# First transfers issued in halves from two queues, and two score steps as 64 by 64 products

## The chip, the cores and the metric

The kernel runs on one core of one Trainium2 chip. The time is the device time of one execution in microseconds (us); several runs are taken and their median is given. One execution is also recorded by the hardware profiler, and all rows below are from that recording. Engines are named as in the profile: PE is the matrix engine, PEld its weight loads, DVE, ACT and POOL the vector, scalar and GpSimd engines, SP the engine that issues the transfers (SPq in the rows).

## The reference, cut to what matters

A decayed linear attention is followed by two pairs of dense layers. Only the attention is touched by the change.

```python
# q, k, v: (2, 8, 768, 64); gamma has one value a head
state = zeros((B, H, D, D))
for t in range(S):
    state = gamma * state + einsum('bhd,bhe->bhde', k[:, :, t], v[:, :, t])
    y[:, :, t] = scale * einsum('bhd,bhde->bhe', q[:, :, t], state)
x = y as (1536, 512)
h = x @ w1_in;  x = (h * tanh(softplus(h))) @ w1_out     # 512 -> 2048 -> 512
h = x @ w2_in;  out = (h * cos(h)) @ w2_out
```

## The kernel before

The recurrence is computed in 12 chunks of 128 positions (6 for each of the 2 batches), all 8 heads of a chunk together. One chunk's input is a row block of 128 partitions by 2048 columns of f32, 1 MB: columns 0 to 1023 hold q and k transposed ("qk", 512 KB; partitions 0 to 63 belong to one head of each pair, 64 to 127 to the other), 1024 to 1535 hold v and 1536 to 2047 hold k (256 KB each). For chunk g PE has four steps, written here with a letter and the chunk's number:

- S(g), `att_scores`, L329: 8 products of 64 by 128 weights with 128 columns, the scores of all heads. PE runs an f32 product in two passes, so that the rows count 16. Two products run side by side, on the upper and the lower half of the array.
- O(g), `att_out`, L384: the masked scores `p` (DVE, L336) times v.
- U(g), `att_update`, L345: k times the decayed v, `vd`, into the running state. `vd` is made by POOL (L305) for chunks 0, 3, 6, 8 and 10 and by ACT (L308, 8 instructions) for 1, 2, 4, 7 and 9.
- I(g), `att_inter`, L374: the state of the chunk before times the decayed q, `qd` (POOL, L313 and L316), as 64 by 64 products, four side by side.

PE's order is fixed by hand: 24 products with zeros (L794) that keep it at work while the first data come, S(0), 8 more products with zeros, S(1), O(0), U(0), S(2), O(1), I(1), S(3), U(1), O(2), I(2), U(2), S(4), O(3), U(3), I(3), S(5) and so on. At the end of the chunks stand O(9), U(9), I(9), S(11), O(10), U(10), I(10), O(11), I(11), and then the first products of the dense layers (L431). The order of SP's transfers is fixed by hand too. The first ones are the constants (146 KB, L765; DVE grows the mask of `p` from them, POOL the factors of `qd`), qk of chunk 0, v0, qk1, k0, qk2, v1, qk3, k1; from there on v and k of a chunk come in one transfer of 512 KB. Each transfer counts on one of 8 semaphores, in turn. The order on DVE, ACT and POOL is made by a small planner (`Plan.order`) from estimated costs; a transfer's cost there is 0.00142 us a column for chunks 0 to 2.

Of the kernel before, what the change touches and what calls it, by code (L numbers as in the profile page):

```python
# [10 lines left out]
F32 = mybir.dt.float32  # L11
F32R = mybir.dt.float32r
# [6 lines left out]
B, H, S, D = 2, 8, 768, 64  # L19
DM, DFF = 512, 2048  # L20
C = 128
# [3 lines left out]
BLK = 512  # L25
# [8 lines left out]
IN_G = (8, 9)  # L34
H_ATT = {(0, 0, 0): "s", (0, 1, 0): "h0", (0, 0, 1): "y", (0, 1, 1): "h0"}
VD_ACT = (1, 2, 4, 7, 9)
ST_ACT = (7, 9)
QD_DVE = ()

# [32 lines left out]
class Plan:  # L72
# [15 lines left out]
    def op(self, engine, cost, fn, *args, needs=(), uses=(), new=None):  # L88
        n = len(self.ops)
        uses = list(uses)  # L90
        before = set(needs)
        reuse = None
        if new is not None:
            key, bufs, *tag = new
            line = self.lines.setdefault(tag[0] if tag else key[0], [])
            if line:
                before.add(self.owner[line[-1]])
            if len(line) >= bufs:
                reuse = line[-bufs]
            line.append(key)  # L100
            self.owner[key] = n
            uses.append(key)
        for key in uses:
            if self.owner.get(key, n) != n:
                before.add(self.owner[key])
            self.users.setdefault(key, set()).add(n)
        if engine in self.given:
            before |= {self.last[engine]} if engine in self.last else set()
            self.last[engine] = n
        att = fn.__name__.startswith("att") or fn.__name__ in ("start_up", "zeros", "load_consts")  # L110
        self.ops.append(dict(engine=engine, cost=cost, fn=fn, args=args, before=before, reuse=reuse, att=att))
        return n
# [64 lines left out]
def retention_two_mlps(ctx: ExitStack, tc: tile.TileContext, qkv, w1i, w1o, w2i, w2o, consts, out):  # L177
    nc = tc.nc
# [6 lines left out]
    g_p = ctx.enter_context(tc.tile_pool(name="g", bufs=3))  # L185
# [81 lines left out]
    att = {}  # L267
# [10 lines left out]
            x_t[m, j] = x_p.tile([128, 2, KD, BLK], F32R, tag="x", name="x")  # L278
        return x_t[m, j]

    def att_load(g, lo, hi, eng=nc.sync):
        if not att:
            t = x_p.tile([128, 2, KD, BLK], F32R, tag="x", name="qkv")
            for n in range(2):
                att[n] = t[:, n].rearrange("p a b -> p (a b)").bitcast(F32)
        elif g in IN_WO and g not in att:
            t = wo_p.tile([128, 2, 2, 512], F32R, tag="wo", name="qkv")
            att[g] = t.rearrange("p a b c -> p (a b c)").bitcast(F32)
        elif g in IN_G and g not in att:
            t = g_p.tile([128, 2, 2, BLK], F32R, tag="g", name="qkv")  # L290
            att[g] = t.rearrange("p a b c -> p (a b c)").bitcast(F32)
        elif g not in att:
            att[g] = att_p.tile([128, 2048], F32, tag="qkv", name="qkv", bufs=3)
        eng.dma_start(out=att[g][:, lo:hi], in_=qkv[g, :, lo:hi])  # L294

    def qk_of(g):
        return att[g][:, 0:1024].rearrange("p (a q b) -> p a q b", a=NPAIR, q=2)

    def att_vd(g, part):
# [3 lines left out]
        d = decv[:, g % NCH, :]  # L303
        if g not in VD_ACT:
            nc.gpsimd.tensor_mul(out=vd[g], in0=v, in1=d.unsqueeze(2).to_broadcast([128, H, D]))  # L305
# [13 lines left out]
    def att_scores(g):  # L319
        qk = qk_of(g)  # L320
        if g == 1:
            both = ps_p.tile([128, 2, NPAIR, C], F32, tag="y", name="ps_s")
            ss = [both[:, e] for e in range(2)]
        else:
            ss = [ps_p.tile([128, NPAIR, C], F32, tag="s", name="ps_s", bufs=3) for _ in range(2)]
        for a in range(NPAIR):
            for e in range(2):
                h = slice(D * e, D * e + D)
                nc.tensor.matmul(ss[e][:, a, :], qk[h, a, 1, :], qk[h, a, 0, :], start=True, stop=True)  # L329
        s_t[g] = ss  # L330

    def att_mask(g, e):
# [17 lines left out]
    def att_state(g):  # L350
        state[g] = att_p.tile([128, NPAIR, D], F32, tag="st", name="st")
        u, by = total[g // NCH], back[:, g % NCH, :]
        if g not in ST_ACT:
            nc.vector.tensor_mul(out=state[g], in0=u, in1=by.unsqueeze(2).to_broadcast([128, NPAIR, D]))
# [180 lines left out]
    op = plan.op  # L535
# [48 lines left out]
    def chunk(g):  # L584
        return ("qkv", max(g, 1))

    def chunk_loads(g, cuts, queue=nc.sync):
        key = chunk(g)
        for lo, hi in zip(cuts, cuts[1:]):
            n = op(  # L590
                "SP", (hi - lo) * (0.00142 if g < 3 else 0.00122), att_load, g, lo, hi, queue,
                uses=[key], new=None if key in plan.owner else (key, 3, "x" if g < 2 else "wo" if g in IN_WO else "g" if g in IN_G else "qkv"),
            )
            for part, last in (("qk", 1024), ("v", 1536), ("k", 2048)):
                if lo < last and hi > last - 512:
                    at.setdefault((part, g), []).append(n)

    def chunk_pre(g):
        c = g % NCH
        key = chunk(g)  # L600
        on_act = g in VD_ACT
        if c + 1 < NCH:
            at["vd", g] = [
                op(
                    *(("ACT", 0.98) if on_act else ("POOL", 1.15)), att_vd, g, part, needs=at["v", g] + at["dec"],
                    new=None if part else (("vd", g), 2), uses=[key, ("vd", g)],
                )
                for part in range(2 if on_act else 1)
            ]
        if c > 0:  # L610
            name, cost, eng = ("DVE", 0.72, nc.vector) if g in QD_DVE else ("POOL", 1.95, nc.gpsimd)
            at["qd", g] = op(
                name, cost, att_qd, g, eng, needs=at["qk", g] + at["decq"], new=(("qd", g), 2), uses=[key]
            )
# [4 lines left out]
    def chunk_scores(g):  # L619
        s = [("s", g, e) for e in range(2)]  # L620
        if g == 1:
            s = [("s", g)] * 2
            at["s", g] = op("PE", 1.05, att_scores, g, needs=at["qk", g], new=(s[0], 1, "y"), uses=[chunk(g)])
        else:
            first = op(None, 0.0, nothing, new=(s[0], 3, "s"))
            at["s", g] = op("PE", 1.05, att_scores, g, needs=at["qk", g] + [first], new=(s[1], 3, "s"), uses=[chunk(g), s[0]])
        for e in range(2):
            at["p", g, e] = at["p", g] = op(
                "DVE", 0.71, att_mask, g, e, needs=[at["s", g]] + at["mask"],
                new=None if e else (("p", g), 2), uses=[s[e], ("p", g)],  # L630
            )

    def chunk_update(g):
        c = g % NCH
        if c + 1 == NCH:
# [6 lines left out]
        at["st", g] = op(  # L642
            *(("ACT", 1.0) if g in ST_ACT else ("DVE", 0.43)), att_state, g, needs=[at["u", g]], new=(st, 2), uses=[u],
        )
# [106 lines left out]
    few_t = []  # L751
# [7 lines left out]
        late_h_p = ctx.enter_context(tc.tile_pool(name="late_h", bufs=1, space=PSUM))  # L759
        o_p = ctx.enter_context(tc.tile_pool(name="o", bufs=2, space=PSUM))  # L760

    def load_consts():
        t = g_p.tile([128, 2, 2, BLK], F32R, tag="g", name="few").rearrange("p a b c -> p (a b c)").bitcast(F32)
        few_t.append(t)
        nc.sync.dma_start(out=t[:, 0:292], in_=consts[:, 0:292])  # L765

    def few(lo, n):
        return few_t[0][:, lo : lo + n]
# [22 lines left out]
    def zeros(n, tag):  # L791
        ps = ps_p.tile([128, 256], F32, tag=tag, name="ps_w")
        for _ in range(n):
            nc.tensor.matmul(ps, zero, zero[:, 0:1].to_broadcast([128, 256]), start=True, stop=True)  # L794

    def start_up():
        nc.vector.memset(zero, 0.0)
        nc.vector.memset(quarter, 0.25)
        nc.vector.memset(magic, MAGIC)
        nc.scalar.activation(out=spare, in_=quarter, func=AF.Copy, scale=quarter)  # L800
        zeros(2 * WARM, "u")

    at["close"] = op(None, 0.0, close)
    op("PE", 5.5, start_up)
    load = op("SP", 0.4, load_consts, new=("few", 3, "g"))
    chunk_loads(0, (0, 1024))
    for g in range(2):
        chunk_loads(g, (1024, 1536))
        chunk_loads(g + 1 + g, (0, 1024))
        chunk_loads(g, (1536, 2048))  # L810
        if g == 0:
            chunk_loads(2, (0, 1024))

    def later_loads(gs):
        for g in gs:
# [30 lines left out]
    for n in range(2):  # L846
        chunk_pre(n)
        chunk_scores(n)
        if n == 0:
            op("PE", 0.9, zeros, 8, "u")  # L850
    for n in range(NCHK):
        if 0 < n < NCHK - 1:
            chunk_pre(n + 1)
# [116 lines left out]
```

## Time and profile before

| what | us |
|---|---|
| median of 3 runs (571.49 to 572.43) | 571.52 |
| the profiled execution's own time | 571.26 |
| its span, first to last instruction | 569.5 |
| its mean granted PE clock, as a share of full speed | 1.000 |

The span of the recording is shorter than the execution's time by what lies before the first and behind the last instruction. Sums that are made on the recording are set against 571.26.

### The profile page before, as it was taken

Reading aid. Unit: us, or ns where it says so; the run is one execution under the profiler, and the core shown is the slowest. Engines: PE = TensorE matmul, PEld = TensorE weight load, DVE = VectorE, ACT = ScalarE, POOL = GpSimd, SP = SyncE. Lnnn points to the kernel's source line nnn. Section 1 sums busy time; section 2 is a strip of 40 time slices with the busy share of each in tenths; the row PEclk is TensorE's granted clock in tenths of the full one; section 3 lists DMA queues with packets and bytes.
Section 4 is the critical chain, followed back from the end, with each engine's and each line's share of the span. In section 5 each row is a group of like instructions: output and inputs, shape, how many; then the busy total and the mean of one; then the engine's idle time right before and its main releaser. Section 6 shows DMA issues by size and latency. Waiting matters only on the chain.

```text
span 569.5 us, 7240 instructions
## 1 busy us (share of the span) xinstructions
PE 565.0 (99%) x3052; PEld 469.0 (82%) x3052; DVE 384.4 (67%) x420; ACT 226.8 (40%) x268; POOL 97.7 (17%) x74
## 2 busy tenths in 40 slices
PE   8999999999999999999999999999999999999997
PEld 6888888888888888888888888888888888888886
DVE  6689899652465527563487976898498894765462
ACT  2565443331312302304326466366246354354240
POOL 6770001111110201111101111122010311010000
PEclk9999999999999999999999999999999999999999
DMA  8982154421042200312022120303004100000203
GB/s 295 403 352 83 70 218 148 148 103 46 1 147 75 74 1 7 142 74 75 0 75 75 48 100 1 147 1 147 1 0 148 39 36 1 0 1 0 75 37 112
DMA packets 15008, 49.90 MB, mean 88 GB/s; under 512 B 1664, under 2 KB 2048, under 8 KB 14976
## 3 DMA queue, kind: packets, MB, share of 16 engines
q1 hardware_dynamic: 14976, 49.44, 23.6%
q8 instruction: 24, 0.39, 0.3%
q14 instruction: 8, 0.07, 0.0%
HBM read 46.29 MB, written 3.15 MB: 87 GB/s over the span
## 4 chain that ended last, share of the span: by engine, by line
PE 98%; DMA 1%; SPq 0%; DVE 0%; issue 0%
PE ps_h L431 46%; PE ps_o L454 46%; PE ps_y L384 2%; PE ps_s L329 2%; DMA qkv<-qkv_dram 1%; PE ps_y L374 1%; PE ps_u L345 1%; SPq L294 0%; DVE acc L520 0%; SPq L765 0%
## 5 line engine op out<-in xcount | busy, mean ns | idle before, releaser
L431 PE MATMUL ps_h<-x,wi 128*128 128x512 f32 x1152 | 264.8, 389 | 0.0
L431 PEld LDWEIGHTS ps_h<-x,wi 128*128 128x128 f32 x1152 | 216.2, 188 | 45.0 <-issue 0.2
L454 PE MATMUL ps_o<-wo,g 128*128 128x512 f32 (+1 forms) x588 | 132.5, 385 | 0.0
L454 PE MATMUL ps_o<-g,wo 128*128 128x512 f32 x576 | 132.4, 389 | 0.0
L454 PEld LDWEIGHTS ps_o<-wo,g 128*128 128x128 f32 x588 | 108.9, 188 | 22.0
L454 PEld LDWEIGHTS ps_o<-g,wo 128*128 128x128 f32 x576 | 108.1, 188 | 22.4
L262 POOL TENSOR_TENSOR wo<-mag,wo 128x1024 fp32r<-128x1024 f32 x14 | 35.8, 2559 | 211.4 <-ACT wo L248 158.4
L497 DVE TENSOR_TENSOR g<-mish,g 128x1024 fp32r<-128x1024 f32 x24 | 33.4, 1393 | 55.0 <-ACT g L493 55.0
L513 DVE TENSOR_TENSOR acc<-ps_o,acc 128x1024 f32<-128x1024 f32 x35 | 42.8, 1222 | 34.6 <-PE ps_o L454 34.4
L262 POOL TENSOR_TENSOR wi<-mag,wi 128x1024 fp32r<-128x1024 f32 x12 | 30.3, 2526 | 193.1 <-ACT wi L248 193.1
L464 ACT ACTIVATE mish<-ps_h 128x1024 f32<-128x1024 f32 (+1 forms) x25 | 24.9, 995 | 95.7 <-PE ps_h L431 95.7
L477 DVE SCALAR_TENSOR_TENSOR turns<-whole,turns 128x1024 f32<-128x1024 f32 x24 | 29.3, 1223 | 44.7 <-ACT whole L473 44.7
L469 ACT ACTIVATE turns<-ps_h,quarter 128x1024 f32<-128x1024 f32 x24 | 26.7, 1113 | 65.4 <-PE ps_h L431 65.1
L239 DVE SCALAR_TENSOR_TENSOR mag<-raw,mag 128x1024 uint32<-128x1024 uint32 (+1 forms) x38 | 42.2, 1111 | 1.2
L486 ACT ACTIVATE turns<-turns 128x1024 f32<-128x1024 f32 x24 | 25.5, 1062 | 34.8 <-DVE turns L483 34.6
L497 DVE TENSOR_TENSOR g<-turns,g 128x1024 fp32r<-128x1024 f32 x24 | 33.2, 1383 | 8.0 <-ACT g L493 8.0
L489 DVE TENSOR_TENSOR turns<-turns,ps_h 128x1024 f32<-128x1024 f32 x24 | 29.2, 1216 | 10.1 <-ACT turns L486 6.8
L254 DVE SCALAR_TENSOR_TENSOR mag<-raw,mag 128x1024 uint32<-128x1024 uint32 x26 | 33.8, 1301 | 0.4
L493 ACT CAST g<-turns 128x1024 fp32r<-128x1024 f32 x24 | 25.1, 1045 | 17.0 <-DVE turns L489 16.8
L248 ACT CAST wi<-mag 128x1024 fp32r<-128x1024 f32 (+1 forms) x20 | 17.4, 872 | 26.5 <-DVE mag L254 22.4
L473 ACT ACTIVATE whole<-turns,magic 128x1024 f32<-128x1024 f32 x24 | 27.7, 1153 | 0.8
L483 DVE TENSOR_SCALAR turns<-turns 128x1024 f32<-128x1024 f32 x24 | 27.0, 1126 | 0.8
(50 smaller groups left out, 326.6 us busy)
## 6 DMA issues: line engine op xcount, KB each, us to landing
qkv<-qkv_dram SPq DMA_DIRECT2D x22, 512.0 KB, 10.0
raw<-w1i_dram SPq DMA_DIRECT2D x16, 512.0 KB, 4.2
raw<-w1o_dram SPq DMA_DIRECT2D x16, 512.0 KB, 4.1
raw<-w2i_dram SPq DMA_DIRECT2D x16, 512.0 KB, 3.7
raw<-w2o_dram SPq DMA_DIRECT2D x16, 512.0 KB, 3.7
out_dram<-acc SPq DMA_DIRECT2D x11, 256.0 KB, 2.1
qkv<-qkv_dram SPq DMA_DIRECT2D x4, 256.0 KB, 7.1
out_dram<-acc SPq DMA_DIRECT2D x2, 128.0 KB, 1.7
```

Of the source, the lines that this page charges most:

```text
L239: nc.vector.scalar_tensor_tensor(out=a, in0=high, scalar=0xC0000000, in1=a, op0=ALU.bitwise_and, op1=ALU.bitwise_or)
L254: nc.vector.scalar_tensor_tensor(out=w_all_of(it, single)[:, ns], in0=raw_t[it][:, ns, :, 0], scalar=29, in1=mag_t[it][:, ns], op0=ALU.log ...
L262: eng.tensor_sub(out=w[:, :, 1], in0=w_all_of(it, single)[:, ns].bitcast(F32), in1=w[:, :, 0].bitcast(F32))
L431: nc.tensor.matmul(h[:, 0 if h_tag(k) == "s" else f % 2, :], w[:, f % 2, a, kk * 128 : (kk + 1) * 128], x[:, b, kk, :], start=(a + b + kk ...
L454: nc.tensor.matmul(ps, lhs, rhs, start=(n == 0), stop=(n == 3 * GF - 1))
L469: nc.scalar.activation(out=t_t[k], in_=h_t[k], func=AF.Identity, scale=INV_2PI, bias=quarter)
L473: nc.scalar.activation(out=n_t[k], in_=t_t[k], func=AF.Identity, bias=magic)
L477: nc.vector.scalar_tensor_tensor(out=t, in0=n_t[k], scalar=MAGIC, in1=t, op0=ALU.subtract, op1=ALU.subtract)
L483: nc.vector.tensor_scalar(out=t, in0=t, scalar1=-0.5, scalar2=0.5, op0=ALU.max, op1=ALU.min)
L489: nc.vector.tensor_mul(out=t_t[k], in0=t_t[k], in1=h_t[k])
L497: nc.vector.tensor_sub(out=g[:, :, 1, :], in0=t_t[k], in1=g[:, :, 0, :].bitcast(F32))
L513: nc.vector.tensor_add(out=acc, in0=o_t[m * NG + G, j, p], in1=acc)
```

## The change

- The constants and qk of chunks 0, 1 and 2 are each loaded by two transfers, one for partitions 0 to 63 (UPPER, issued by SP) and one for 64 to 127 (LOWER, issued by ACT). k0 as a whole is issued by ACT too. ACT issues its five in `start_up`, ahead of its first activation: constants, qk0, qk1 (LOWER each), k0, qk2 (LOWER).
- SP's order is now: constants, qk0, qk1 (UPPER each), v0, qk2 (UPPER), v1, qk3, k1. So v0 stands behind qk1, where it stood ahead of it.
- The planner's cost of these transfers is 0.0013 us a column, halved for a half.
- S(0) and S(11) are 16 products of 64 by 64 weights, the keys in two halves, in the order in which all four quarters of the array are used in turn.
- 4 products with zeros, not 8, stand between S(0) and S(1).

```diff
+SQUARE = (0, 11)
...
-    def att_load(g, lo, hi, eng=nc.sync):
+    early = []
+    issued = set()
+    EVERY, UPPER, LOWER = slice(0, 128), slice(0, 64), slice(64, 128)
+
+    def att_load(g, lo, hi, eng=nc.sync, at_rows=EVERY):
...
-        eng.dma_start(out=att[g][:, lo:hi], in_=qkv[g, :, lo:hi])
+        if (g, lo, hi, at_rows) not in issued:
+            eng.dma_start(out=att[g][at_rows, lo:hi], in_=qkv[g, at_rows, lo:hi])
+            issued.add((g, lo, hi, at_rows))
...
         for a in range(NPAIR):
-            for e in range(2):
-                h = slice(D * e, D * e + D)
-                nc.tensor.matmul(ss[e][:, a, :], qk[h, a, 1, :], qk[h, a, 0, :], start=True, stop=True)
+            for keys in (slice(0, D), slice(D, C)) if g in SQUARE else (slice(0, C),):
+                for e in range(2):
+                    h = slice(D * e, D * e + D)
+                    nc.tensor.matmul(
+                        ss[e][keys, a, :], qk[h, a, 1, keys], qk[h, a, 0, :], start=True, stop=True, skip_group_check=True,
+                    )
...
-                "SP", (hi - lo) * (0.00142 if g < 3 else 0.00122), att_load, g, lo, hi, queue,
+                "SP", (hi - lo) * (0.0013 if g < 3 else 0.00122) * share, att_load, g, lo, hi, queue, at_rows,
...
+            if queue is not nc.sync:
+                early.append((g, lo, hi, queue, at_rows))
...
     def start_up():
+        load_consts(nc.scalar, LOWER)
+        for load in early:
+            att_load(*load)
         nc.vector.memset(zero, 0.0)
...
-    chunk_loads(0, (0, 1024))
     for g in range(2):
-        chunk_loads(g, (1024, 1536))
-        chunk_loads(g + 1 + g, (0, 1024))
-        chunk_loads(g, (1536, 2048))
-        if g == 0:
-            chunk_loads(2, (0, 1024))
+        chunk_loads(g, (0, 1024), at_rows=UPPER)
+        chunk_loads(g, (0, 1024), nc.scalar, LOWER)
+    chunk_loads(0, (1024, 1536))
+    chunk_loads(0, (1536, 2048), nc.scalar)
+    chunk_loads(2, (0, 1024), at_rows=UPPER)
+    chunk_loads(2, (0, 1024), nc.scalar, LOWER)
+    chunk_loads(1, (1024, 1536))
+    chunk_loads(3, (0, 1024))
+    chunk_loads(1, (1536, 2048))
...
         if n == 0:
-            op("PE", 0.9, zeros, 8, "u")
+            op("PE", 0.45, zeros, 4, "u")
```

## Rows read from the trace of the kernel before

**Rows 1.** The page: what each engine was busy, and the chain's shares.

```profile
PE 565.0 (99%) x3052; PEld 469.0 (82%) x3052; DVE 384.4 (67%) x420; ACT 226.8 (40%) x268; POOL 97.7 (17%) x74
...
PE 98%; DMA 1%; SPq 0%; DVE 0%; issue 0%
```

**Rows 2.** The chain in order of time: start, length, what.

```profile
2.10 6.57 DMA qkv<-qkv_dram
...
8.71 1.16 PE ps_s L329 x16
...
38.45 0.60 PE ps_y L374 x16
39.05 1.09 PE ps_s L329 x16
```

**Rows 3.** Timeline of the first 11 us: start, length, instructions, [idle before <- releaser].

```profile
5.86 0.27 PE L794 MATMUL ps_w<-zero 128*128 128x256 bf16 x1
...
6.07 1.16 PE L329 MATMUL ps_s<-qkv 64*128 64x128 f32 x16
7.16 1.06 PE L794 MATMUL ps_w<-zero 128*128 128x256 bf16 x8
```

**Rows 4.** Timeline of the first 11 us, the other engines.

```profile
7.26 1.29 DVE L336 TENSOR_TENSOR p<-ps_s,cst 128x512 f32<-128x512 f32 x2 [0.26 <-PE ps_s L329]
7.44 1.04 POOL L305 TENSOR_TENSOR vd<-qkv,cst 128x512 f32<-128x512 f32 x1
...
10.62 0.60 PEld L345 LDWEIGHTS ps_u<-vd,qkv 128*64 128x64 f32 x16
...
10.94 0.58 ACT L398 CAST x<-ps_y 128x512 fp32r<-128x512 f32 x1 [8.63 <-PE ps_y L384]
```

**Rows 5.** Transfers: SP's issues of v0, k0, qk2 and v3 with k3.

```profile
1.64 0.42 SPq L294 DMA_DIRECT2D qkv<-qkv_dram  x1
...
2.58 0.43 SPq L294 DMA_DIRECT2D qkv<-qkv_dram  x1
3.05 0.58 SPq L294 DMA_DIRECT2D qkv<-qkv_dram  x1
...
8.69 0.33 SPq L294 DMA_DIRECT2D qkv<-qkv_dram  x1
```

**Rows 6.** Transfers, size and us to landing: v0, k0, qk2; the constants; later weights.

```profile
qkv<-qkv_dram SPq DMA_DIRECT2D x1, 256.0 KB, 5.2
qkv<-qkv_dram SPq DMA_DIRECT2D x1, 256.0 KB, 6.7
qkv<-qkv_dram SPq DMA_DIRECT2D x1, 512.0 KB, 7.5
few<-consts_dram SPq DMA_DIRECT2D x1, 146.0 KB, 2.3
raw<-w1i_dram SPq DMA_DIRECT2D x16, 512.0 KB, 4.2
```

**Rows 7.** Stretches: busy time of each engine; last the clock, DMA share, GB/s.

```profile
2.00:8.00 6.00, 6.00 (x45) 4.32 (x42) 4.43 (x11) 0.31 (x2) 4.38 (x10) 1.00 0.94 274
8.00:10.00 2.00, 1.51 (x22) 1.17 (x22) 0.63 (x2) 0.00 (x0) 1.59 (x3) 1.00 1.06 420
10.00:20.00 10.00, 10.00 (x200) 8.81 (x198) 7.84 (x14) 5.59 (x19) 7.42 (x11) 1.00 1.02 392
20.00:30.00 10.00, 10.00 (x201) 8.75 (x199) 6.83 (x13) 4.76 (x15) 8.18 (x12) 1.00 1.03 410
```

**Rows 8.** Timeline around U(7): ACT's `vd` of chunk 7 and the step that reads it.

```profile
29.47 2.02 ACT L308 ACTIVATE vd<-qkv,cst 128x64 f32<-128x64 f32 x8 [1.44 <-DMA qkv<-qkv_dram]
...
31.46 0.63 PE L345 MATMUL ps_u<-vd,qkv 128*64 128x64 f32 x16
```

**Rows 9.** I(9), the first round and the first three rounds of four 64 by 64 passes.

```profile
38.38 0.34 PE L374 MATMUL ps_y<-qd,st 64*64 64x128 f32 x4
...
38.38 0.56 PE L374 MATMUL ps_y<-qd,st 64*64 64x128 f32 x12
```

More of the change, by code (lines that the diff above doesn't have):

```diff
@@ L585, in chunk, with chunk_loads @@
         return ("qkv", max(g, 1))
-    def chunk_loads(g, cuts, queue=nc.sync):
+    def chunk_loads(g, cuts, queue=nc.sync, at_rows=EVERY):
         key = chunk(g)
+        share = (at_rows.stop - at_rows.start) / 128
         for lo, hi in zip(cuts, cuts[1:]):
             n = op(
-                "SP", (hi - lo) * (0.00142 if g < 3 else 0.00122), att_load, g, lo, hi, queue,
+                "SP", (hi - lo) * (0.0013 if g < 3 else 0.00122) * share, att_load, g, lo, hi, queue, at_rows,
                 uses=[key], new=None if key in plan.owner else (key, 3, "x" if g < 2 else "wo" if g in IN_WO else "g" if g in IN_G else "qkv"),
             )
+            if queue is not nc.sync:
+                early.append((g, lo, hi, queue, at_rows))
             for part, last in (("qk", 1024), ("v", 1536), ("k", 2048)):
@@ L760, in close, with load_consts @@
         o_p = ctx.enter_context(tc.tile_pool(name="o", bufs=2, space=PSUM))
[L762 to L765, printed above, removed]
+    def load_consts(eng=nc.sync, at_rows=UPPER):
+        if not few_t:
+            t = g_p.tile([128, 2, 2, BLK], F32R, tag="g", name="few")
+            few_t.append(t.rearrange("p a b c -> p (a b c)").bitcast(F32))
+        eng.dma_start(out=few_t[0][at_rows, 0:292], in_=consts[at_rows, 0:292])
     def few(lo, n):
```

## The prediction

> **What bounds the kernel now.** I read the page first: PE is busy for 99% of the span, and the chain that ended last runs on PE for 98% of it [rows 1]. Next the chain in order of time: ahead of S(1) it follows a transfer, qk1, that was issued at 2.10 and takes 6.57 us; from S(1) at 8.71 on it never leaves PE until the last accumulation [rows 2]. So the 557.8 us from 8.71 to the end of PE's work are PE's own steps without a gap, and a change of the first transfers can win only (a) what starts S(1) and the steps behind it earlier, and (b) what shortens a step. Then the timeline of the start says what else stands ahead of S(1): the last warming product starts at 5.86, S(0) at 6.07, the 8 zero products at 7.16, ending at 8.22 [rows 3]; PE then waits about half a microsecond for qk1. Last come the transfers and the places later on where something with a time of its own, and not one that follows PE, just makes it.
>
> **The change part by part.**
>
> *Zeros and S(0).* The zero products take (1.06 - 0.27)/7 = 0.113 us each at this place [rows 3]; four fewer are 0.45 us. S(0) itself can hardly move: the warming products end where they did, the last begins at 5.86, and whatever qk0's landing adds is within the 0.2 us from there to 6.07. As squares (below) it is 0.05 shorter. So PE could begin S(1) at 8.22 - 0.45 - 0.05, about 7.7, a full microsecond earlier, if its data were there.
>
> *qk1.* In the order of before, 146 + 512 + 256 + 512 KB = 1426 KB stand up to and with qk1; it lands at 2.10 + 6.57 = 8.67 [rows 2]. v0 (914 KB) lands at 1.64 + 5.2 = 6.84, k0 (1682 KB) at 2.58 + 6.7 = 9.28, qk2 (2194 KB) at 3.05 + 7.5 = 10.55 [rows 5, 6]. In the new order v0 is behind, so that 1170 KB stand up to and with qk1. Read off the same curve between 6.84 and 8.67 this is 7.75. With 0.04 us from landing to PE, S(1) begins at about 7.8, 0.9 earlier.
>
> *v0.* This is the price, and it takes most of that back. v0 is now served side by side with k0 behind 1170 KB: its last byte is between 1426 KB (8.67, if it is served first) and 1682 KB (9.28, if the two take turns to the end). I take 9.2, near the second, since the two stand in different queues. Behind v0 hangs POOL's `vd` of chunk 0, which takes 1.04 us [rows 4] and which U(0) reads. In before it was far ahead of U(0), whose weights start to load at 10.62 [rows 4]. Now it is late next: 9.2 + 0.1 + 1.04 + 0.1 = 10.44, so U(0) moves up by only 0.18. With 9.28 it is 0.10; with 8.67 `vd` would be ready at 9.9, and PE's own steps (S(1) at 7.8, 1.16 to O(0) by rows 2, then O(0)) put U(0) at about 10.0, 0.65 earlier. The mask is no limit: `p` of chunk 0 is ready at 7.26 + 1.29 = 8.55 [rows 4], ahead of O(0) at 8.95 or later. Behind `vd` on POOL stands `qd` of chunk 1, pushed back too, but I(1) has room for it: S(2) and O(1) come first.
>
> *The stream of transfers later on.* From 10 us on they move 392 to 410 GB/s with the transfer engines busy all the time [rows 7], so that a landing there is a matter of bytes before it, and from qk2 on the bytes before each transfer are what they were. A step that reads such data can come earlier only by its slack. The tightest that I find is U(7): ACT begins `vd` of chunk 7 when its transfer lands, at 29.47, and has the last of 8 heads at 31.49; U(7) runs from 31.46 to 32.09 and needs that head in its second half [rows 8]. That leaves about 0.2 us. A PE that is 0.2 us ahead just passes; one that is a microsecond ahead is held there, unless the whole stream has moved up.
>
> *Does the stream move up?* From 2 to 8 us it moved 274 GB/s, against 420 from 8 to 10 [rows 7]: at 410 from the start, (6 x (410 - 274))/410 = 2.0 us less. If the slow start were a matter of issuing, two queues would mend it. It does not look so: qk1 is in the queue by 2.53 [rows 5] and lands at 8.67. [...]
>
> *Issue.* ACT has nothing of the chain to do before 10.94 [rows 4], so its five issues, about 0.45 each by SP's [rows 5], 2.2 us in all, are hidden; they would cost from the moment they ran past 10.94. On SP the issues stay short, but an issue waits for the eighth before it: 8.69 stands 0.02 behind the landing of qk1 [rows 5, 2]. ACT's five come first in the count, so v0 waits for the LOWER constants (2.3 us to landing [rows 6], so about 3), qk2 UPPER for qk0 LOWER (about 6), v1 for qk1 LOWER (7.75), qk3 for k0 (9.3). Queued behind on SP are all later chunks. With 4.2 us from issue to landing of a lone 512 KB [rows 6], qk2 would be there at 10.2 and qk3 at 13.5, about when they were; some 768 KB still under way cover the gap. I take it at nothing; without that cover S(2) or S(3) waits some tenths.
>
> *S(11) as squares.* It stands behind I(9), which is made of 64 by 64 products already. I(9) takes 0.60 and S(11) 1.09 to the next start [rows 2]. A further round of four 64 by 64 passes takes (0.56 - 0.34)/2 = 0.11 [rows 9]; S(11) is 8 such rounds, 0.88 if it follows without a break, 0.21 less than now. If it had to start anew as I(9) does, 0.60 + 4 x 0.11 = 1.04, 0.05 less. I take 0.21, since I(9) shows that such rounds follow one another. For S(0), which stands between products of another shape, it is the 0.05 from above, and hidden while S(1) waits for its data.
>
> **The sum.** S(1) could win 0.9, U(0) keeps 0.18, U(7) lets about 0.2 through: -0.2. S(11): -0.2. Together -0.4: 571.26 - 0.4 = 570.9 for a profiled execution. The median of the runs is 0.26 above the profiled one, so 571.52 - 0.4 = **571.1**.
>
> **The rivals.**
>
> 1. *The start gets faster.* The two queues keep the transfer engines as busy from 2 us as from 10. Then qk1 is there by 7.7, v0 well before 8.55, the stream moves up by up to 2.0 and U(7) with it; PE's own steps are the limit: -1.0 for S(1), -0.2 for S(11), 570.3. For it: 274 against 410 GB/s, and shares of the transfer engines below one (0.94) in that stretch. Against it: issuing is long done, and the bytes are the same. Half a gain (0.5 to 0.9) belongs here too.
> 2. *It is hidden anyway.* v0 lands at 9.4, U(0) stays where it was, squares win 0.05: 571.5, no change. For it: the curve gives 9.28, only 0.1 off.
> 3. *Slower: v0 comes late.* Every microsecond by which v0 lands behind 9.4 is one on the path, by POOL's `vd` of chunk 0 and U(0). If transfers of 64 partitions moved a quarter slower in the start, 2 + 1.25 x (9.28 - 2) = 11.1: U(0) at 12.3, 1.7 later, less 0.2 of S(11): +1.5, 573.0. It gets slower by over 0.2% from a landing at about 10.8. Against it: k0 with half of qk2's bytes lands 0.6 us behind qk1, qk2 1.3 behind k0, so smaller transfers as such are no slower; a transfer of half the partitions the trace does not have. [...]
>
> **How the numbers follow.** Forecast (-0.05 to -0.7 around -0.4) 0.55; rival 1, 0.17, of which 0.10 reach 0.2%; rival 2, 0.19; rival 3, 0.09, of which 0.07 pass 0.2%. I use 0.2%, 1.14 us, as about what a measurement of this kernel can tell from no change. The whole possible gain, 1.2 us, just passes that. So faster 0.10, same 0.83, slower 0.07. The range reaches from rival 1's 570.3, with 0.2 for the scatter of the runs, to +0.5 of a mild rival 3: 570.1 to 572.0.
>
> **What would show it.** In the profile after: S(1) near 7.8, behind 4 zero products and a short wait on qk1. U(0) should wait on POOL's `vd`, which itself waited for v0 until about 9.2; a U(0) at 10.0 would show v0 served first, one behind 10.6 the slower case. Transfers from 2 to 8 us near 274 GB/s; near 400 would be the first rival. U(7) should be at or near the end of ACT's `vd`. I(9) and S(11) should take 1.48 together instead of 1.69. The prediction is wrong if the stretch from S(1) to the end has shrunk by more than the 0.2 of S(11), if PE has found a new wait behind U(0), or if the planner's other order on DVE, ACT or POOL makes PE wait in the dense layers, where it never did.

## The result: 0.6% slower

The changed kernel took 575.02 us in the median of 6 runs (574.68 to 575.64), the kernel before 571.61 (571.44 to 572.62, 6 runs beside it). The ratio is 1.0056, with a 95% interval from 1.0044 to 1.0069. The forecast was 571.1, in a range up to 572.0. The profiled execution took 574.96 against 571.26, 3.70 more.

The page of the profile after. PE is still busy for 99% of the span, but 3% of the chain that ended last are now transfers, where it was 1% [rows 1]:

```profile
PE 564.8 (99%) x3080; PEld 468.6 (82%) x3080; DVE 385.1 (67%) x420; ACT 226.9 (40%) x268; POOL 98.0 (17%) x74
...
PE 96%; DMA 3%; ACTq 0%; DVE 0%; issue 0%; SPq 0%
```

The chain of the profile after, in order of time (start, length, what), to be laid beside [rows 2]:

```profile
2.23 7.22 DMA qkv<-qkv_dram
...
9.46 0.33 SPq L300
...
9.84 8.68 DMA qkv<-qkv_dram
...
18.56 1.09 PE ps_y L394 x16
...
20.25 0.75 PE ps_u L355 x16
...
41.58 0.60 PE ps_y L384 x16
42.17 0.87 PE ps_s L337 x32
...
44.54 0.37 PE ps_y L384 x7
44.91 0.18 issue
45.09 0.54 PE ps_y L384 x9
...
47.25 0.90 PE ps_h L441 x3
```

The same chain in the kernel before, at O(2) and at the first products of the dense layers, and the transfer of v2 and k2 there, which was issued at 6.01 (size, us to landing):

```profile
15.78 0.88 PE ps_y L384 x16
...
43.85 32.86 PE ps_h L431 x144
```

```profile
qkv<-qkv_dram SPq DMA_DIRECT2D x1, 512.0 KB, 8.3
```

Before, PE never had to wait again once it had started S(1). Now it waits at O(2), 18.56, for the transfer of v2 and k2, which was issued at 9.84 and lands at 18.52. From there on it runs through as before, 3.1 us late, up to S(11) at 42.17 (39.05 before [rows 2]). S(11) took 0.87 to the next start instead of 1.09. Then, in I(10), stands a break in which PE waited for nothing that the profile shows; with it I(10) took 1.09 instead of 0.60. The first product of the dense layers starts at 47.25, where it was 43.85.

The timeline of PE in the start of the profile after, and POOL's `vd` of chunk 0, beside [rows 3, 4]:

```profile
5.86 0.43 PE L337 MATMUL ps_s<-qkv 64*64 64x128 f32 x2 [0.79 <-DMA qkv<-qkv_dram]
8.06 1.10 PE L337 MATMUL ps_s<-qkv 64*64 64x128 f32 x30 [1.78 <-DMA qkv<-qkv_dram]
9.10 0.62 PE L808 MATMUL ps_w<-zero 128*128 128x256 bf16 x4
9.64 1.16 PE L337 MATMUL ps_s<-qkv 64*128 64x128 f32 x16
10.73 1.09 PE L394 MATMUL ps_y<-p,qkv 128*64 128x128 f32 x16
12.73 0.69 PE L355 MATMUL ps_u<-vd,qkv 128*64 128x64 f32 x16 [0.91 <-DMA qkv<-qkv_dram]
```

```profile
10.40 1.05 POOL L312 TENSOR_TENSOR vd<-qkv,cst 128x512 f32<-128x512 f32 x1 [2.56 <-DMA qkv<-qkv_dram]
```

S(0) ran its first two passes on the UPPER half of qk0 and then waited 1.78 us for the LOWER one. POOL waited for v0, and U(0) waited for k0. Of the row blocks that the steps wait for, each is complete later than before: qk0 at 8.02 (6.00 before), qk1 at 9.45 (8.67), v0 at 10.33 (6.81), k0 at 12.60 (9.32). The reason shows in the stretches of the profile after (busy time of each engine; last the clock, DMA share, GB/s; the share adds up the times of the packets and can pass one), beside [rows 7]:

```profile
2.00:8.00 6.00, 3.50 (x23) 2.37 (x20) 3.69 (x9) 1.58 (x2) 3.85 (x9) 1.00 0.94 219
8.00:10.00 2.00, 1.94 (x40) 1.53 (x42) 0.80 (x2) 0.00 (x0) 0.00 (x0) 1.00 1.07 260
10.00:20.00 10.00, 8.64 (x160) 7.35 (x156) 6.40 (x11) 4.59 (x16) 7.52 (x10) 1.00 1.02 351
20.00:30.00 10.00, 10.00 (x205) 8.57 (x195) 6.93 (x12) 4.19 (x15) 7.60 (x11) 1.00 1.03 413
```

And 8 to 13 us, while most of the halves are under way, first the kernel before, then the change:

```profile
8.00:13.00 5.00, 4.51 (x78) 3.98 (x78) 3.35 (x6) 2.06 (x8) 4.28 (x7) 1.00 1.04 407
```

```profile
8.00:13.00 5.00, 4.03 (x75) 3.29 (x77) 2.58 (x4) 0.59 (x1) 2.45 (x3) 1.00 1.05 249
```

The transfer engines were as busy as before (shares of 0.94 and 1.07, before 0.94 and 1.06), and moved fewer bytes: 260 GB/s in 8 to 10, where it was 420. PE's granted clock is 1.00 in all these stretches, so the clock is no part of it. The last half lands at 13.58, and from 13 us on the rate is the old one (398 from 13 to 20, 389 before).

**Where the 3.70 us are.** v2 with k2 landed 4.2 later than before (18.52 against 14.3); O(2) had 1.4 of slack, so it moved by 2.78 (18.56 against 15.78 in the chain before). ACT's `vd` of chunk 2 starts at that landing too and makes U(2) late by another 0.35. S(11) gives back 0.21. The break in I(10) costs 0.49. The last 0.30 lie behind the last product, in the store of the result.

Of the 4.2 us by which v2 with k2 is late, 2.9 are the stream's: k1, the transfer ahead of it, is 2.85 late (15.96 against 13.11) and the one behind it 3.2. The other 1.3 stand beside a packet of 16 KB of the instruction queue (16.39 to 17.48 in the trace's transfer records): v2 with k2 lands 2.55 behind k1, where such transfers follow one another by 1.2 to 1.3. Before, that packet (13.73 to 14.68) came a transfer later, and the one behind v2 with k2 landed 2.18 after it and had the slack for it. In all 17 traces the first or second landing behind the end of the first such packet, 0.7 to 2.2 us behind it, stands 1.6 to 2.8 us behind the one ahead of it. That the packet causes this no run here shows, and such gaps occur without one too. It moves the place of the loss more than its size: the transfer of chunk 7 is 3.1 late in any case, and an estimate from that and from U(7)'s slack of 0.2 [rows 8] is a loss of 2.9 there. In the kernel with the change's transfers only, below, v2 with k2 landed at 17.21, while the packet was still under way, O(2) did not wait for it, and the dense layers still began 3.0 later than before.

### The profile page after: what moved, and what is told of

It is laid out like the page before. It is cut to its first block, busy times and chain, and to the rows that moved or that the text cites. A ratio compares the mean times of both kernels' runs of the same rounds, so it can differ in the third digit from the quotient of the medians.

```text
span 573.2 us, 7303 instructions
## 1 busy us (share of the span) xinstructions
PE 564.8 (99%) x3080; PEld 468.6 (82%) x3080; DVE 385.1 (67%) x420; ACT 226.9 (40%) x268; POOL 98.0 (17%) x74
## 4 chain that ended last, share of the span: by engine, by line
PE 96%; DMA 3%; ACTq 0%; DVE 0%; issue 0%; SPq 0%
PE ps_h L441 46%; PE ps_o L464 46%; DMA qkv<-qkv_dram 3%; PE ps_y L394 2%; PE ps_s L337 1%; PE ps_y L384 1%; PE ps_u L355 1%; ACTq L300 0%; ACTq L779 0%; DVE acc L530 0%; SPq L300 0%
## 5 line engine op out<-in xcount | busy, mean ns | idle before, releaser
L249 ACT CAST wi<-mag 128x1024 fp32r<-128x1024 f32 (+1 forms) x20 | 17.5, 873 | 26.6 <-DVE mag L255 22.4
```

## The experiments

All times are medians, each with its ratio to runs of the kernel before on the same chip (571.6 to 571.9). GB/s are those of the profiled execution in three stretches; the last column is the landing of v2 with k2 there.

| kernel | us (runs) | ratio, 95% interval | 2:8 | 8:10 | 13:20 | v2 with k2 |
|---|---|---|---|---|---|---|
| before | 571.6 | | 274 | 420 | 389 | 14.3 |
| the change | 575.02 (6) | 1.0056, 1.0044 to 1.0069 | 219 | 260 | 398 | 18.5 |
| halves, one queue | 575.54 (4) | 1.0069, 1.0046 to 1.0092 | 203 | 227 | 367 | 19.1 |
| halves by columns | 574.64 (4) | 1.0049, 1.0033 to 1.0064 | 235 | 409 | 332 | 15.3 |
| squares only | 572.30 (10) | 1.0011, 1.0001 to 1.0021 | 278 | 388 | 411 | 15.1 |
| order, whole, one queue | 572.15 (10) | 1.0005, 0.9995 to 1.0014 | 228 | 425 | 399 | 15.2 |
| the change's transfers only | 574.62 (4) | 1.0045, 1.0032 to 1.0059 | 219 | 249 | 394 | 17.2 |
| even and odd partitions | 573.10 (8) | 1.0021, 1.0010 to 1.0031 | 252 | 411 | 413 | 17.1 |
| S(11) alone | 571.74 (11) | 0.9999, 0.9990 to 1.0007 | 278 | 411 | 416 | 16.0 |
| squares, 8 zeros | 572.07 (11) | 1.0003, 0.9995 to 1.0012 | 288 | 392 | 412 | 15.2 |
| qk2 in two halves | 573.51 (10) | 1.0032, 1.0019 to 1.0045 | 298 | 246 | 404 | 16.2 |
| qk2 in four quarters | 574.10 (6) | 1.0041, 1.0027 to 1.0056 | 292 | 245 | 397 | 15.6 |
| squares S(9) to S(11) | 573.04 (12) | 1.0015, 1.0005 to 1.0025 | 268 | 376 | 415 | 15.7 |
| even and odd, one queue | 575.04 (4) | 1.0054, 1.0038 to 1.0069 | 216 | 378 | 387 | 17.5 |
| weights by row ranges | 572.33 (1) | | 262 | 417 | 416 | 16.4 |
| whole, two queues | 572.98 (10) | 1.0022, 1.0009 to 1.0034 | 317 | 416 | 390 | 13.5 |
| v0 and k0 from ACT | 571.56 (11) | 0.9999, 0.9990 to 1.0008 | 310 | 399 | 396 | 14.4 |

**Which part costs: queues, halves, order or squares.** Three kernels undo one part of the change each, and a fourth has the squares and the 4 zeros alone. The theories were: W, transfers of 64 partitions are slow; Q, two queues served by turns are; S, SP's late issues are.

```diff
-        chunk_loads(g, (0, 1024), nc.scalar, LOWER)
+        chunk_loads(g, (0, 1024), nc.sync, LOWER)      # all halves, and k0, from SP
```

> The changed kernel with the LOWER halves and k0 issued by SP, next to their UPPER halves, and nothing by ACT. Theory W (transfers into 64 partitions move slowly, whoever issues them): the stretch from 2 to 13 us still moves about 240 GB/s, v2 with k2 lands near 18, the time is about 574 to 576. Theory Q (two queues that take turns on the same transfer engines slow each other): from 8 us on about 410 GB/s, v2 with k2 lands near 14.5, about 571.5. Theory S (SP's issues come late, since they wait for the landing of the eighth before): also near 571.5, with the issues of v1, qk3 and k1 by 6 us.

```diff
-        chunk_loads(g, (0, 1024), at_rows=UPPER)
-        chunk_loads(g, (0, 1024), nc.scalar, LOWER)
+        chunk_loads(g, (0, 512))                       # halves by columns
+        chunk_loads(g, (512, 1024), nc.scalar)
```

> The changed kernel with qk of chunks 0 to 2 cut by columns and not by partitions: 128 partitions of 512 columns from SP and as many from ACT; the constants whole, from SP. Queues, counts and order stay. Theory W: about 400 GB/s from 6 us on, v2 with k2 near 14.5, about 571.3. Theory Q: as slow as the change, about 240 GB/s to 13 us, 574 to 576. Theory S: slow by the gaps behind SP's waits alone; the rate is full while both queues have work, about 572 to 573.

```diff
+SQUARE = (0, 11)                                       # on the kernel before
...
-            op("PE", 0.9, zeros, 8, "u")
+            op("PE", 0.45, zeros, 4, "u")
```

> The kernel before with the 64 by 64 products for chunks 0 and 11 and 4 zero products, transfers untouched. All theories: S(1) still waits for qk1 until 8.7; S(11) takes 0.88 behind I(9), so 571.6 - 0.2 = 571.4. If the squares or the fewer zeros carry the loss, it is 573 or more; a break of about 0.5 us in I(10), as in the changed kernel, would show that this belongs to the squares and not to late data.

```diff
-        chunk_loads(g, (0, 1024), at_rows=UPPER)
-        chunk_loads(g, (0, 1024), nc.scalar, LOWER)
+        chunk_loads(g, (0, 1024))                      # whole, all from SP, order of the change
```

> Whole transfers, SP alone, in the changed order (qk0, qk1, v0, k0, qk2, v1, qk3, k1), squares and 4 zeros. The working of the prediction without its halves: S(1) near 7.8, v0 near 8.7 to 9.3, U(0) 0.1 to 0.6 earlier, v2 with k2 near 14.3, about 571.1. If the order itself were the loss: U(0) behind 10.7 and 572 or more.

Halves from one queue are as slow as from two, so Q falls. S falls with it: SP had issued v1 and qk3 by 7.86 there, and from 8 to 10 us full transfer engines (share 1.07) moved 227 GB/s. Whole transfers in the new order, with the squares, are within 0.1% of before, so the loss is in the halves, and the new order has won nothing: qk1 landed at 8.80 there, although v0's 256 KB no longer stood ahead of it. That execution had a slow start, though (228 GB/s from 2 to 8): qk2, with the same bytes ahead of it as before, landed 0.8 late as well (11.37 against 10.56). The squares alone were forecast at 571.4 and took 572.30, 0.1% above before: their trace has a break in I(10) again, of 0.37. Halves by columns kept the full rate from 8 us on (409) and were slow for another reason. Both queues served qk0 among the rest, and its second half came at 7.85; PE idled 1.82 us ahead of S(0), its granted clock fell (0.66 from 8 to 13), and S(1) took 2.01 us instead of 1.09. The stretch of the kernel with halves by columns, clock third from the end:

```profile
8.00:13.00 5.00, 5.00 (x68) 4.14 (x70) 3.02 (x5) 0.00 (x0) 3.29 (x4) 0.66 1.05 406
```

Next, the transfers of the change without its squares, and the squares without its transfers:

```diff
-SQUARE = (0, 11)                                       # on the change
+SQUARE = ()
...
-            op("PE", 0.45, zeros, 4, "u")
+            op("PE", 0.9, zeros, 8, "u")
```

> The transfers of the change (halves of 64 partitions on two queues, the new order) with the score steps and the zeros of before. Theory W (while halves of 64 partitions are under way, the full transfer engines move some 40% fewer bytes, so that v2 with k2 lands near 18.5 and O(2) waits for it): 2:8 near 220 and 8:13 near 250 GB/s, O(2) near 18.6, and the time 2.9 to 3.3 above before, some 574.7, since S(11) gives nothing back. Theory P (the square products set the loss, by PE's shape changes in the start or by PE's own instructions coming late): under 572.5. The break of PE in I(10) should be gone or stand elsewhere if it hangs on the number of PE instructions ahead of it.

```diff
+SQUARE = (11,)                                         # on the kernel before
```

> Transfers and zeros of before; only S(11) is made of squares. If the gain of S(11) stands, 0.2 below before: 571.4. If the break of PE behind it (0.3 to 0.7 us in I(10) where both steps were squares) is a matter of where PE's instructions come from, it moves by the 8 to 12 instructions that are fewer ahead of it, and the time is 571.4 to 572.2.

```diff
+SQUARE = (0, 11)                                       # on the kernel before, 8 zeros kept
```

> Transfers of before, both steps as squares, 8 zeros as before. S(1) at 8.7 to 8.85, since it waits for its data anyway. If the break of PE hangs on the count of PE instructions ahead of it, it stands 4 products earlier than with 4 zeros, at the start of I(10) or in U(10); if it hangs on the moment, it stays about 44 to 45 us. The time 571.3 to 572.3.

The transfers alone cost 2.9 us, as W had it. Only the place moved: the chain of that execution goes over v0, which landed at 12.26, and O(0) waited for it:

```profile
2.89 9.37 DMA qkv<-qkv_dram
...
12.40 1.09 PE ps_y L394 x16
```

S(11) alone gained nothing that can be measured, though it took 0.87 in the profile too; in that execution O(2) waited 0.3 for v2 with k2, which landed at 15.96, 2.5 behind k1 and behind an instruction packet that ended at 14.92. The breaks of PE are taken up below.

**Why halves are slow.** The same two halves as even and odd partitions, from two queues and from one:

```diff
-    EVERY, UPPER, LOWER = slice(0, 128), slice(0, 64), slice(64, 128)
+    EVERY, UPPER, LOWER = slice(0, 128), slice(0, 128, 2), slice(1, 128, 2)
```

> The change as it is, but with the halves as the even and the odd partitions: again 64 partitions to a transfer, the same bytes, queues and order, but spread over all 128. [...] Theory W2 (few rows to a transfer cost, wherever they lie, since each then goes to fewer engines or in other pieces): as slow as the change, 8:13 near 250 GB/s, the time 574.5 to 575.5.

> The even and odd partitions again, all issued by SP, in order. They left 1.4 us of the loss with two queues. If that rest comes from the two queues (SP waits for a landing before it issues v2 with k2, and the halves of qk0 and qk1 land side by side with others): 571.9 to 572.4, the time of whole transfers in this order. If it comes from the transfers being halves (more and shorter ones in the start): again 572.8 to 573.4.

In 8 to 10 us both moved 411 and 378 GB/s, against 260 and 227 for neighbours: the number of partitions is not what cost, but which they were, and W2 falls. The times did not follow the rate: 573.1 and 575.0. From two queues O(2) waited 1.5 us for v2 with k2. The chain of that kernel:

```profile
8.61 8.46 DMA qkv<-qkv_dram
...
17.12 1.09 PE ps_y L394 x16
```

k1 had landed at 14.32, 1.2 later than before; v2 with k2 came 2.75 behind it, again behind an instruction packet (14.89 to 15.82). At the usual 1.2 to 1.3 it would have been there at 15.6, in time for O(2): in the one execution recorded, the rest of the loss hangs on this gap. From one queue the odd half of qk0 landed at 7.84, PE idled 2.04 us ahead of S(0) and the granted clock was 0.66 from 8 to 13, S(1) again 2.01 long; that fits the late qk0 of the halves by columns, not W. That kernel also has a slow stretch from 10 to 13 us (225 GB/s at a share of 0.97), which I can't explain. The halves don't show in it: from 7.84 on they and v0 and k0, 256 KB each, land 0.6 to 0.7 us apart up to the last half at 11.70; it is the whole transfers behind them, v1 and qk3, that take until 13.32 and 15.64.

Then a dose: one transfer of the kernel before, qk2, in halves and in quarters.

```diff
-        eng.dma_start(out=att[g][:, lo:hi], in_=qkv[g, :, lo:hi])
+        for r in range(0, 128, 64 if (g, lo) == (2, 0) else 128):      # 32 for quarters
+            rows = slice(r, r + (64 if (g, lo) == (2, 0) else 128))
+            eng.dma_start(out=att[g][rows, lo:hi], in_=qkv[g, rows, lo:hi])
```

> The kernel before, with one single transfer changed: qk2 (512 KB) as two transfers of partitions 0 to 63 and 64 to 127, both from SP. A third of the bytes that the change moves in halves. Theory W (a range of 64 neighbouring partitions is written at the 249 GB/s of the changed kernel instead of 410): 0.52 MB take 2.1 us instead of 1.3, so the stream behind qk2 is 0.8 later, v2 with k2 lands near 15.2 (hidden, O(2) starts at 15.8), and U(7) with its 0.2 of slack passes on 0.6: 572.3. Theory E (what costs is the first engine-wide start or the use of two queues, not the halves): 571.7, no change.

> The same single transfer as four of 32 neighbouring partitions each. [...] Theory N (the rate falls in proportion to the number of neighbouring partitions): half of the rate of the halves, 4.2 us for qk2, the stream 2.9 later, 574.4. Theory D (each further transfer has a price of its own): twice to three times what the two halves cost over before.

In both the rate fell while qk2 was under way, to 246 and 245 GB/s, and the last part of qk2 landed at 11.35 in both (10.6 before): 32 neighbours were no slower than 64 (P in the run with the weights below), and N falls. The profiled execution of the halves took 572.24, and 572.3 was the forecast; but v2 with k2 landed at 16.22 instead of 15.2 (2.4 behind k1, an instruction packet having ended at 14.27), and O(2), which was to be untouched, waited 0.4. The ten runs reach from there to 575.83, and the medians are 1.2 (halves) and 1.8 (quarters) above those 572.3, so the size of the dose is not shown by the times. In the recorded execution of the quarters (573.84) O(4) waited 0.48 for a transfer that landed at 22.80, 2.8 behind the one ahead of it, 1.7 us after the next instruction packet; S(8) waited for ACT's work on weights that landed at 29.20 (26.86 before). The other executions were not recorded.

Last, the same question where nothing else moves. The weights of the dense layers come in pairs of 512 KB; here they are split in three ways.

```diff
+PARTS = {
+    "i0": (slice(0, 128),),                                    # w1i
+    "o0": (slice(0, 64), slice(64, 128)),                      # w1o
+    "i1": (slice(0, 128, 2), slice(1, 128, 2)),                # w2i
+    "o1": (slice(32, 96), slice(0, 32), slice(96, 128)),       # w2o
+}
...
-            nc.sync.dma_start(out=to, in_=of)
+            for rows in PARTS[it[0] + str(m)]:
+                nc.sync.dma_start(out=to[rows], in_=of[rows])
```

> A measurement on the kernel before, away from the start: the weights of the dense layers come in pairs of 512 KB transfers when nothing else moves, w1i whole as before, w1o as partitions 0 to 63 and 64 to 127, w2i as even and odd partitions, w2o as 32 to 95, then 0 to 31 and 96 to 127. Theory W with P (a range of 64 or 32 neighbours inside one half of the partitions is written at some 250 GB/s, a range with as many partitions from both halves at full rate): the pair of w1o lands some 1.8 us later than a whole pair (1.05 MB at 249 instead of 410 is 4.2 us instead of 2.6), w2i's no later than 0.3, and of w2o the 32 to 95 part runs at full rate and the two others at the slow one. Theory H (64 partitions are slow whichever they are; even and odd ones were quick for another reason): w2i and w2o as late as w1o. Theory S (it belongs to the start alone): all as whole. The time itself 571.4 to 572.4, since the weights have slack there.

Stretches of 7 or 8 us with one pair of 1.05 MB in each, so that the share of the transfer engines' time that the pair took can be compared. The whole pair of w1o, in the profile of the kernel before:

```profile
81.00:89.00 8.00, 8.00 (x37) 6.62 (x36) 7.53 (x12) 4.12 (x5) 0.00 (x0) 1.00 0.35 131
```

The split weights: w1o in halves, w2i even and odd, w2o with its middle half in one piece:

```profile
81.00:89.00 8.00, 8.00 (x37) 6.62 (x36) 7.49 (x14) 3.42 (x5) 0.00 (x0) 1.00 0.54 131
...
292.00:299.00 7.00, 7.00 (x32) 5.79 (x32) 6.05 (x7) 1.77 (x2) 0.00 (x0) 1.00 0.46 152
300.00:308.00 8.00, 8.00 (x37) 6.63 (x36) 4.76 (x3) 5.25 (x5) 2.48 (x1) 1.00 0.50 132
```

For the same bytes the engines need 0.35 x 8 = 2.8 us for whole transfers, 0.54 x 8 = 4.3 for halves of neighbours, 0.46 x 7 = 3.2 for even and odd partitions. w2o, half of it in partitions 32 to 95 and half in the two outer quarters, needs 4.0, and in two other pairs 3.6 and 3.9; the middle between whole and halves is 3.6. So the slowness is not of the start, it went with the range: 131/0.54 = 243 GB/s at full share for partitions 0 to 63 and 64 to 127, 131/0.35 = 374 for all.

The forecast was made of landings, and by them it held in part. From the first issue to the last landing the pair of w1o took 6.7 us (4.4 whole), 2.3 more where 1.8 was forecast; w2i 1.1 more (5.5, whole 4.4) where 0.3 was, as SP needs 0.6 us for each of its four issues; w2o as much as w1o (2.2 more), so that its landings don't show 32 to 95 to be quick. The single packets of 4 KB, one partition's row each, do. In order of their starts, the third 64 packets of a pair (the third transfer of a split pair, if the queue keeps its order) take 159 to 161 ns in the median in whole pairs, in w2i and in all six pairs of w2o, where they are the second 32 to 95, and 287 to 308 in w1o. This also answers a rival: 64 neighbours are read from rows that follow one another in the source, and even or odd ones are not; but 32 to 95 follow one another too, and are quick.

So in these runs the rate went by which partitions a transfer covered: 64 neighbours from 0 or from 64 on were slow (243 GB/s at full share against 374), quarters of 32 like halves (245 and 246 in 8 to 10 us), even and odd ones near whole (3.2 us a pair against 2.8), 32 to 95 quick by their packets (159 to 161 ns). Why it is so no trace here shows.

**Is there anything in a second queue?** Two kernels keep it and drop the halves:

```diff
-    for g in range(2):                                 # on the change
-        chunk_loads(g, (0, 1024), at_rows=UPPER)
-        chunk_loads(g, (0, 1024), nc.scalar, LOWER)
+    chunk_loads(0, (0, 1024))
+    chunk_loads(1, (0, 1024), nc.scalar)               # qk2 whole from ACT too, constants from SP
```

> The change without its halves: constants, qk0, v0, v1, qk3, k1 whole from SP, qk1, k0, qk2 whole from ACT, both score steps as squares and 4 zeros. If the halves are what costs, 3 us of the 3.4 come back: 571.6 to 572.4, with 8:13 near 410 GB/s. If two queues side by side cost something of their own (qk1 from ACT is served beside qk0, which then lands late, PE idles in the start and its granted clock falls), 573 to 575.

```diff
+    chunk_loads(0, (1024, 1536), nc.scalar)            # v0, beside k0; the rest whole from SP
...
-SQUARE = (0, 11)
+SQUARE = ()
```

> What the runs so far point to: whole transfers, constants, qk0, qk1, qk2, v1, qk3, k1 from SP, v0 and k0 from ACT behind its first activation, so that they don't push qk0 back; no square steps, 4 zeros. Theory R (a second queue keeps the transfer engines busier in the start, 317 against 274 GB/s, so that the whole stream is ahead): 2:8 above 300 GB/s, qk0 near 6, qk1 by 8.3, S(1) 0.4 earlier, v2 with k2 by 14: 570.9 to 571.5. Theory T (the bytes of the two queues are served by turns, so that what one transfer wins another loses): qk1 no earlier than 8.7 or qk0 late as in the two-queue run before it (7.8), 571.7 to 573.

The first 6 us moved more here, 317 and 310 GB/s, where the eight recorded executions with SP alone and the first transfers of before moved 262 to 298; v2 with k2 landed 0.8 earlier in the first. With one execution each, that two queues raise the rate is likely and not shown. Neither kernel is faster than before. In the first, qk1 from ACT was served ahead of qk0. The chain of that kernel:

```profile
1.18 6.60 DMA qkv<-qkv_dram
...
7.82 1.10 PE ps_s L337 x32
```

Five of its ten executions, with a granted clock of 0.999 or 1.000 over the span, took 572.3 to 572.5; the five with 0.996 or 0.997 took 573.5 to 574.5. In the second, ACT issued v0 and k0 from 0.99 on, ahead of its first activation and so earlier than meant; qk0 landed at 6.58, qk1 at 8.45, and S(1) began 0.2 earlier. The gain was lost at S(8). The chain of that kernel shows what it waited for: a transfer of weights that lands at 27.33, ACT's `mag` made from it, ACT's `x` queued behind that, and DVE's `p` of chunk 7 behind `x`:

```profile
16.91 10.42 DMA raw<-w1i_dram
...
27.35 0.68 ACT mag L217
28.03 0.48 ACT x L408
...
29.14 0.69 DVE p L346
...
29.88 1.16 PE ps_s L337 x14
```

So R's rate was there, and the time is that of before. No version that I ran beats the kernel before.

**PE's breaks.** Three square steps:

```diff
+SQUARE = (9, 10, 11)                                   # on the kernel before
```

> Transfers and zeros of before; S(9), S(10) and S(11), all behind an I step and behind U(7), as squares. Each should save 0.22 on PE: 0.66, 571.1. Against it: squares double the number of PE's instructions in these steps, and PE has stood without an instruction for 0.3 to 0.9 us shortly after a packet of the instruction queue in the kernels with two square steps. If such breaks come here they take back half or more: 571.4 to 572.2.

S(9) and S(11) took 0.87 each, and yet the kernel lost 1.2 us in the median, more than the forecast allowed (571.1, or 571.4 to 572.2 with breaks). Its chain:

```profile
33.41 0.87 PE ps_s L331 x32
...
36.38 0.21 PE ps_s L331 x5
36.59 0.65 issue
37.23 1.09 PE ps_s L331 x27
...
42.31 0.11 PE ps_u L349 x3
42.41 0.49 issue
42.90 0.62 PE ps_u L349 x13
```

With their breaks S(10) took 1.95 and U(10) 1.22, where 0.87 and 0.47 would do: 1.8 us more against 0.66 saved. (The recorded execution had lost another 0.7 ahead of S(9).) PE stood twice without an instruction and resumed, each time 1.2 to 1.3 us after a packet of 16 KB of the instruction queue had ended (35.94 and 41.66 in the trace's transfer records). In the other kernels with such breaks PE resumed 1.3 to 1.6 after one. Eight of the ten kernels with two or three square steps have them, and none of the seven with one or none. The place goes by the count of PE's instructions, not by the time: in the change, in "squares only" and in "halves by columns" the break in I(10) comes after 7 of its 16 passes, at 44.91, 42.47 and 44.72; with 4 more zeros in the start ("squares, 8 zeros") it comes after 3, four earlier, as forecast. Breaks in S(10) go the same way: after 9 passes with 4 zeros ("halves by columns", "order, whole, one queue" and "whole, two queues"; 7 in "even and odd, one queue"), after 5 with 8 zeros ("squares, 8 zeros" and the three squares). The break in I(10) with 8 zeros:

```profile
42.49 0.36 PE ps_y L378 x3
42.84 0.32 issue
43.17 0.66 PE ps_y L378 x13
```

In the "S(11) alone" kernel the 16 KB packets come 6.4 us apart in the mean (first at 13.95, fifth at 39.69), in which PE takes (203 + 198) x 0.64 = 257 instructions (products and weight loads in 20 to 30 us of that kernel). The kernel before has them too, from 13.73 to 40.02, and there PE had no break.

So I read it thus: PE's instructions come with these packets, and a square step, 32 passes where there were 16, saves 0.22 and uses them up sooner than the next packet brings more. This is an estimate from the places, which go by the count, and from the 1.2 to 1.6 us behind a packet; what a packet holds no trace shows. That the packet comes late because the transfer engines are full was not tried.

## Why the prediction was wrong

The step that failed is "Does the stream move up?". It asked whether two queues would raise the rate, took qk1's 2.53 against 8.67 for a no, and left the rate as it was: the loss of rate stood in the sum at nothing, without a row for a transfer of half the partitions. The halves of qk0 landed one behind the other (UPPER at 5.8, LOWER at 8.0). But while halves were under way the rate was not that of whole transfers: 249 GB/s instead of 407 from 8 to 13 us. This is rival 3's mechanism, which had a chance of 0.09 and a price of "a quarter slower", taken as 1.25 times the time for the same bytes; no row showed the quarter, and in the run it was 407/249 = 1.6 times. From 2 to 13 us 6 x (274 - 219) + 5 x (407 - 249) = 1120 KB fewer were moved, 2.8 us of the stream at 400 GB/s; k1 landed 2.85 late.

- **qk1.** Forecast 7.75, measured 9.45. Whether the reading off the curve was right without the halves is open: whole and in the new order qk1 landed at 8.80, but in an execution whose whole stream was 0.8 late, and with the transfers of before it landed anywhere from 7.90 to 8.99.
- **S(0).** "Can hardly move" was wrong: it waited for LOWER until 8.06.
- **v0.** Forecast 9.2; it landed at 10.3 and POOL waited for it, as the step said. U(0) then waited for k0 (12.60), which the step had not looked at. In the transfers-only kernel it was v0 after all.
- **Which landing decides.** Rival 3 put it on v0. In the change it is v2 with k2, whose slack of 1.4 us at O(2) the prediction had not looked for, as it took landings from qk2 on for unchanged. That it was this one is in part the place of an instruction packet, which no step of the prediction had.
- **U(7).** Its 0.2 of slack never came to bear: ACT's `vd` of chunk 7 began at 32.58 and U(7) ran from 34.59, both 3.1 later than [rows 8]. The stream and PE were late by the same.
- **Issue.** ACT's five issues were hidden, as forecast, though they took until 4.53 and not 2.2 us. The count of the semaphores ran through both queues in turn, and not through ACT's five first: v0 was issued at 2.61 without a wait, and v1 at 8.04, behind qk0 LOWER. SP issued v2 with k2 only at 9.84 and the chain names it, but the transfer engines were full throughout (shares of 1.07 in 8 to 10 and 1.02 in 10 to 20), so that this cost nothing that shows.
- **S(11).** Right in size: I(9) and S(11) took 1.47 together, forecast 1.48. What the step left out is that more instructions have a price: the break of 0.49 in I(10).
- **Planner.** The order of instructions on DVE, ACT and POOL did not change, but for ACT's issues.

What stays open: what makes a landing 1 us late behind an instruction packet, why the stretch from 2 to 8 us moves anything from 228 to 298 GB/s with whole transfers from one queue, and the spread of the runs with qk2 split. Only one execution of each was recorded.

## What to carry to other kernels

Before a transfer is split, ask which partitions each part covers: here ranges inside 0 to 63 or 64 to 127 moved their bytes at 61 to 65% of the rate (249 against 407 GB/s in the start, 243 against 374 with the weights), from one queue (230) no faster than from two (249), and the share of the transfer engines (1.05 against 1.04) did not show it, only GB/s beside the share. When a stream is bound by its bytes, look for the slack of every landing and not only of the first ones: here O(2) took 1.4 us off a landing that was 4.2 late, and U(7) would have taken only 0.2 off a stream that was 3.1 late. A step made of more and shorter instructions is to be set against the breaks that come with it: three square steps saved 0.66 here and lost 1.8.

## What the runs showed of the hardware

- Even and odd partitions moved nearly as fast as all 128 (3.2 us of engine time a pair, 2.8 whole, 4.3 for neighbours).
- Two queues moved 317 and 310 GB/s in the first 6 us with whole transfers (one execution each; one queue 262 to 298 in eight), but in their own order: a qk1 issued by ACT landed 2.4 us ahead of the qk0 that SP had issued 0.4 later.
- PE stood still 0.1 to 0.9 us, waiting for nothing that the profile shows, at places that moved with the count of its instructions, and resumed 1.2 to 1.6 us after 16 KB packets of the instruction queue.
- Behind the first 16 KB packet of the instruction queue the first or second landing came 1.6 to 2.8 us after the one ahead of it in all 17 traces, where 512 KB transfers otherwise follow by 1.2 to 1.3.
- A 4 KB packet, one partition's row, took 159 ns in the median in whole transfers and in even and odd ones, 287 to 309 in the later halves of 64 neighbours.
- Where PE had idled 1.82 and 2.04 us ahead of S(0), the granted clock was 0.66 in the mean from 8 to 13 us, and S(1) took 2.01 instead of 1.09 us. Behind an idle stretch of 1.53 us ("whole, two queues") the clock stayed at 1.00.
